# Attention with chunk selection and an MLP on one core: first loads in another buffer, chunk bounds by one strided reduction, another order

## The chip, the cores and the metric

The kernel runs on one core of a Trainium2 chip. The metric is the device time of one execution in microseconds (us). The core has five engines with a queue each: PE (matmuls; its weight loads are shown apart as PEld), DVE (VectorE), ACT (ScalarE), POOL (GpSimd) and SP (SyncE, which here issues DMAs alone). POOL and ACT issue a few DMAs too. Each engine runs its own queue in the order in which the program gives it, and waits at the head of that queue for what an instruction needs.

## What is computed

q, k and v have the shape (4 batches, 8 heads, 768 positions, 64) in float32. The keys are cut into 24 chunks of 32. Of each chunk the smallest and the largest value in each of the 64 dimensions are taken; they give an upper bound of any score in the chunk:

```
k_min, k_max = min / max of k over the 32 keys of a chunk
ub   = sum over d of max(q * k_min, q * k_max)       # chunks after the query's own: -1e9
keep = the 6 chunks of the largest ub for each query
attn = softmax over kept keys, not after the query, of q.k / 8
x    = attn @ v, heads side by side: (3072, 512)
out  = elu(x @ w_in) @ w_out                         # w_in (512, 2048), w_out (2048, 512)
```

## The kernel before, in words

**Work units.** The 3072 tokens are 8 units of 384. Units 0 and 1 hold the first halves of batches 0 and 1, mixed: in the code u = 0 (tags with "p") is the first 192 positions of both batches, u = 1 (tags with "s") is the next 192. Units 2 to 7 are second half of batch 0, second half of batch 1, and the halves of batches 2 and 3. A unit goes through loading, transposes, chunk bounds and selection (`select`), scores, exponentials and the product with v (`attend_pair` for units 0 and 1, `attend` for the others), division by the sum (`divide`) and a transpose (`turn`; a DMA transpose for units 2 to 7). Then `mlp` runs it through both weight matrices: 16 products with w_in of 384 columns (L881, ops h), ELU in three steps on ACT, POOL or DVE, and DVE (L888 e, L890 m, L894 g), and 12 groups of products with w_out (L905, ops o; the last tile at L861).

**The recording layer.** `Graph.op` records operations with the engines that may run them, what they read and write; nothing is issued then. The string ORDER, written out, gives the queue (first letter of a triple: P, A, D, G for POOL, S for SP) and the operation's number; PLACES gives the slot that each buffer takes, in the order of first use. An operation runs on the engine that ORDER names; waits come from what it reads, writes and overwrites. So the two strings fix all queues and all reuse of buffers. PE also gets products of zeros (op fill, L944) at places of ORDER: 40 of them.

**Loads.** `prep_pair` loads k and q of u = 0 and u = 1 and calls `load_v` for v; all of it lands in class f, 8 slots of 128x512 float32 (q and k tiles use 96 rows). `load_v` casts what landed into vext (`vcast`, L335 on POOL, L322 on ACT, L324 on DVE). `prep` loads the later halves: k, q of batches 0 and 1, and v, into f too; q of batches 2 and 3 goes in 32-wide blocks into class fx (4 slots of 128x768 float32), to be transposed by DVE at L589. The weights come through POOL's queue: `load_w_in` (L293, three parts: hidden columns 0 to 3, 4 to 7 and 8 to 15 of 16) and `load_w_out` (L299, four parts), straight into w_in_sb and w_out_sb.

**Chunk bounds.** For batches 0 and 1 keys are transposed on PE (L404, L554), and DVE reduces them in place in PSUM (L369). For batches 2 and 3 `bounds_batch` (its two batches have 8 rounds in all: two head groups times two halves of a chunk each) loads 96 rows, one for each head and chunk, of 16 keys x 64 dimensions into the single buffer kc. DVE then halves the keys: a minimum of 512 against 512 into a buffer t of class f (L486), a maximum of the same in place in kc (L489), then for each of the two a run of 256, 128 and 64 (L495), the last into km. The two halves are joined at L501, maximum less minimum is taken at L504, and a transpose on PE (L508) and copies put them into kst. `select` multiplies kst with q (L609) and finds the six largest on DVE (L620 to L637).

Of the kernel before, what the change touches and what calls it, by code (L numbers as in the profile page):

```python
# [9 lines left out]
AOT = mybir.AluOpType  # L10
# [8 lines left out]
D = 64  # L19
# [20 lines left out]
D01D00S0yG03A0uS0rA0sD09G0jG04S0tP0DS0WP0MD0gA0VA02G06G0iPjVPjXP1aS0vA0HS0xD0OS0ZS0+S0wG0cS0YD0n  # L40
P11G05S0XG0dG07G0-P0KD0ED12G0aA0LPjWG0kA15P0TD0NS2RS0BS2iG0bD1cA0QP1jD0qA0SG0mP1kP1hD1eA0UG0RD0F
PjZD1bS2fPj+A10P1pP1oPjYP18D13S0zPj-S2hA0CPk0Pk1P1uD19G0AP1zP1tD0lGmzP1vG0GD0PD1iA1xS2gPk3P1qPk2
P2JGmAA1rA1sS2QA2KA1wP2wG0pP1lPk4P2oP2BA2xD2CP1yPk6A1mA1nA2LP1DS2IS2vS2kS2OP1APk8A1CP20D2DD2sP1N
D2qD2pPk5A1BP1OP1ED1FP1SD2ND2tG0oGmBP33P29P1RD34G0eP1IP1HD1PP3gG08P1+D2EG2MG2uD1JD1GD1TD1KD1UA0J
PkaPkcP25G17G2AP26G0fP1XA2FA3hD1QD21A2yD27P2aP1LD2bA2HD2cD2zA1gS2PS4-G2rP1YP1VP3lD1ZD1-D28D22A1W
P2dD2ePkeD1MGmCG2SG2GP23A24A1fPmWPmKPm-Pn2D3mD3nD3pAmXAmLD3oGmMA3iD3qDmNAm+An3D3rD3sGn0Dn1G14PmG
PmOPmSPkgPnePnyPk7AmHDmIDn4G3tG0hAmTDmJDmUPnCG2lGmYAmPAnfDn5DmVP38D3vA0IDmQP3+AnzDmRP3JGngGmDAnD
Pk9DnhGmEP4FDnAG3jPn6A3cDnEA40A3KP2XAn7A2+D39S32G3uS2mDnBDmZDnFPnaD3aP3HPnuAnbA3ID2YPnqGn8P4jA4G
D2ZD35D2-PkiG1dD3bPnmAnrA3kG36A4kGnsP3wP41GmFDn9D3yG3eAnvA16G30A42S3fGnwD3xPnGS50P4lAnnA31DntGno
S57A2nP4DPnTD3APkkDnpPnMS4+PniA4mA3dD3LDnxG37PnUPnND3zS2TD3BPnHD3CA4EAnjA3EDncDnkG2jG3DG3GPkbDnl  # L50
P3NDndPkdG43P4aD4nA4bP3QPnID3FP3MP48S7UP3SD3OP4MD3PP44S2VG2UA3TP45PnVA3RD46P5rA4NSbCP4OP5fS4YD47
G4HA4PD5sA2WS4ZP4sD5gD3UA49PnWD4QP4JP4uP4IP4RPnJP3WP3VA5tA4tD3XS4XA4vP5QD3YP4pD4KAnXG4cD4LAnKP4S
P3ZS7LG4wP4oA5RA3-D4TG5TSnYD4qP5EA5FP4eS7IP4dP4yG5vP4xA5SP5xD4UD4fP4VP5kSawA5oD4gP4hSbuA4WPnOD4z
D5yD4rD4AA4iD5zP5JP4BG5qS55P58PkfPkmA5BD5GD5LD5aA4CPoNSavPotD5mPnPS53AouPo9PoFG5AAoOD59D5hD5lD5K
A5HDoPG5bGovG5nD5iAnQS5wD5MAoGA5cDowAoaA5NDoQSaGSnSGobDoHS7KSbrG5eS7SP5VSbzDoIPo5G5jPopA56PnZAo6
# [115 lines left out]
def kernel(  # L171
# [9 lines left out]
    nc = tc.nc  # L181
# [194 lines left out]
    def prep_pair(b, u, G):  # L376
# [617 lines left out]
```

## Time and profile before

| | us |
|---|---|
| median of 3 runs (lowest to highest) | 291.08 (290.72 to 291.61) |
| the profiled execution's own time | 290.3 |
| its span (first to last instruction) | 288.5 |
| PE busy, share of the span | 267.1 (93%) |
| DVE busy | 231.6 (80%) |
| ACT busy | 202.1 (70%) |
| POOL busy | 116.9 (41%) |

Times of the trace count from the start of the span. "x85" in a row is a count of instructions, the two numbers after the bar are the group's busy time in us and the mean of one instruction in ns, and what stands after the second bar is the engine's idle time just before them and what ended it. In rows of the DMA issues, the last number is the median time from issue to landing. The granted TensorE clock is 0.998 of full.

### The profile page before, as it was taken

The numbers are of one execution on the slowest core, as the hardware profiler recorded it, in microseconds if no ns is written. First come the engines' busy times: TensorE is split into PE (matmuls) and PEld (weight loads), VectorE is DVE, ScalarE is ACT, GpSimd is POOL, SyncE is SP. The second block draws the span as 40 slices with busy tenths as digits, with TensorE's granted clock in tenths as the row PEclk, the third lists the DMA queues.
The fourth block names the chain that finished last, engine by engine and source line by source line (L and its number), as shares of the span: only waits on it lengthen the run. The fifth ranks groups of instructions, "written<-read, shape, count | busy, mean of one in ns | idle before, by whom it ended". The sixth has DMA issues, their size and how long they took to land.

```text
span 288.5 us, 6864 instructions
## 1 busy us (share of the span) xinstructions
PE 267.1 (93%) x2404; PEld 161.9 (56%) x2404; DVE 231.6 (80%) x711; ACT 202.1 (70%) x453; POOL 116.9 (41%) x218
## 2 busy tenths in 40 slices
PE   2897889999999999998799999999999999999995
PEld 1565555685546765556465555664555455665553
DVE  2729898769989999999998999899789869442761
ACT  2457579487789889999289559993599259892611
POOL 5448366433844237722056336530556023400210
PEclk9999999999999999999999999999999999999999
DMA  8999999968966569997598268664370240012103
GB/s 162 189 186 202 203 199 197 214 139 189 222 132 134 134 147 215 181 242 144 130 213 186 44 148 202 109 122 97 94 179 2 57 110 0 16 50 66 74 3 109
DMA packets 119715, 39.25 MB, mean 136 GB/s; under 512 B 111104, under 2 KB 115456, under 8 KB 119680
## 3 DMA queue, kind: packets, MB, share of 16 engines
q1 hardware_dynamic: 114256, 34.09, 56.8%
q0 software_dynamic: 3696, 4.19, 8.8%
q10 hardware_dynamic: 1728, 0.52, 0.8%
q8 instruction: 19, 0.31, 0.5%
q14 instruction: 16, 0.13, 0.1%
HBM read 30.41 MB, written 6.29 MB: 127 GB/s over the span
## 4 chain that ended last, share of the span: by engine, by line
PE 52%; DVE 23%; DMA 9%; issue 6%; ACT 4%; POOL 3%; SPq 1%; ACTq 0%; DVEq 0%; POOLq 0%
PE bank L881 19%; PE bank L905 14%; DMA xt<-on 6%; PE bank L791 5%; DVE gT L894 5%; PE bank L842 3%; DVE on L655 3%; PE bank L609 2%; DMA f<-in_k_dram 2%; ACT pt L806 2%; DVE rhs L324 2%; POOL m L890 2%; DVE m L890 2%; DMA f<-in_q_dram 1%; PE bank L404 1%
## 5 line engine op out<-in xcount | busy, mean ns | idle before, releaser
L881 PE MATMUL bank<-xt,w_in_sb 128*128 128x384 bf16 x512 | 91.2, 326 | 4.9 <-DMA xt<-on 3.3
L905 PE MATMUL bank<-w_out_sb,gT 128*128 128x512 bf16 x368 | 90.3, 379 | 0.2 <-DVE gT L894 0.2
L888 ACT ACTIVATE e<-bank 128x384 f32<-128x384 f32 x128 | 60.8, 496 | 41.5 <-PE bank L881 34.1
L890 POOL TENSOR_SCALAR m<-e 128x384 f32<-128x384 f32 x85 | 45.1, 538 | 87.3 <-ACT e L888 77.9
L894 DVE SCALAR_TENSOR_TENSOR gT<-bank,m 128x384 bf16<-128x384 f32 x128 | 66.4, 547 | 11.0 <-POOL m L890 9.6
L881 PEld LDWEIGHTS <-w_in_sb 128*128 128x128 bf16 x512 | 49.5, 98 | 40.7 <-issue 8.8
L806 ACT ACTIVATE pt<-bank 128x384 bf16<-128x384 f32 (+1 forms) x144 | 67.9, 547 | 4.1 <-PE bank L791 3.2
L905 PEld LDWEIGHTS <-gT 128*128 128x128 bf16 x368 | 34.8, 97 | 33.9 <-issue 1.5
L791 PE MATMUL bank<-rhs,lhs 96*128 96x384 bf16 (+2 forms) x240 | 44.4, 293 | 0.3 <-DVE on L655 0.2
L791 PEld LDWEIGHTS <-lhs 96*128 96x128 bf16 x240 | 21.8, 97 | 14.4 <-issue 0.7
L823 POOL TENSOR_TENSOR pt<-pt,tri 128x256 bf16<-128x256 bf16 (+1 forms) x18 | 16.1, 899 | 26.6 <-ACT pt L810 20.2
L842 PEld LDWEIGHTS <-pt 128*128 128x128 bf16 x576 | 21.1, 97 | 4.6 <-DVE pt L823 0.7
L842 PE MATMUL bank<-vext,pt 128*128 128x65 bf16 x576 | 22.6, 193 | 0.6 <-DVE pt L823 0.6
L369 DVE TENSOR_REDUCE kst<-bank 128x12 f32<-128x384 f32 x32 | 16.6, 548 | 7.5 <-PE bank L404 7.3
L890 DVE TENSOR_SCALAR m<-e 128x384 f32<-128x384 f32 x43 | 17.6, 419 | 5.0 <-ACT e L888 4.8
L655 DVE TENSOR_TENSOR on<-bank,rcp 128x384 bf16<-128x384 f32 (+1 forms) x40 | 19.3, 497 | 0.8
L322 ACT ACTIVATE o<-bank 128x512 f32<-128x512 f32 (+1 forms) x16 | 8.7, 559 | 13.4 <-PE bank L905 10.5
L404 PE MATMUL bank<-ident_f,f 96*128 96x96 f32 x64 | 10.7, 313 | 7.6 <-POOL econst L278 4.3
L810 ACT ACTIVATE pt<-bank 128x512 bf16<-128x512 f32 x24 | 14.7, 614 | 1.6 <-PE bank L842 0.8
L404 PEld LDWEIGHTS bank<-ident_f,f 96*128 96x128 f32 x64 | 8.3, 180 | 10.8 <-POOL econst L278 4.3
L823 DVE TENSOR_TENSOR pt<-pt,tri 128x512 bf16<-128x512 bf16 (+1 forms) x30 | 12.6, 438 | 2.0 <-ACT pt L810 1.8
L653 DVE RECIPROCAL rcp<-bank 128x6 f32<-128x6 f32 (+1 forms) x40 | 7.2, 182 | 7.6 <-PE bank L842 3.7
(104 smaller groups left out, 330.3 us busy)
## 6 DMA issues: line engine op xcount, KB each, us to landing
f<-in_v_dram SPq DMA_DIRECT2D x22, 256.0 KB, 4.7
out_dram<-o SPq DMA_DIRECT2D x21, 256.0 KB, 2.5
f<-in_k_dram SPq DMA_DIRECT2D x18, 256.0 KB, 4.9
fx<-in_q_dram SPq DMA_DIRECT2D x32, 96.0 KB, 3.4
kc<-in_k_dram SPq DMA_DIRECT2D x8, 384.0 KB, 4.4
w_out_sb<-in_moe_w_out_dram POOLq DMA_DIRECT2D x4, 512.0 KB, 10.1
f<-in_q_dram SPq DMA_DIRECT2D x6, 256.0 KB, 4.1
f<-in_q_dram SPq DMA_DIRECT2D x6, 192.0 KB, 4.8
```

The costliest lines, as they stand in the source:

```text
L369: g.op(("kmin", "kmax")[w] + tag, (DVE,), lambda e, w=w, op=op: nc.vector.tensor_reduce(out=cs(w), in_=src(), axis=AX.X, op=op), reads=[(b ...
L404: nc.tensor.transpose(ap(bk)[:, c0:c0 + T96], ap(src[j])[0:T96, 256 * G + P * pr:256 * G + P * pr + P], ident_f[0:T96, 0:T96])
L655: g.op("on" + tag, (DVE,), lambda e: nc.vector.tensor_tensor(out=ap(on)[:, 0:nt].rearrange("p q h d -> p h q d"), in0=view()[:, :, :, 0:D] ...
L791: nc.tensor.matmul(ap(banks[hd])[:, o + pc:o + pc + wd], lhsT=apl(ls, G)[0:96, pr, hd, P * kb:P * (kb + 1)], rhs=ap(rs)[0:96, hd, c0 - HS ...
L806: lambda e, hd=hd, pt=pt, banks=banks, wtot=wtot: nc.scalar.activation(out=ap(pt)[:, hd, PAD:PAD + wtot], in_=ap(banks[hd])[:, 0:wtot], fu ...
L823: eng[e].tensor_tensor(out=view, in0=view, in1=tri[:, 64:64 + P].rearrange("p (a b w) -> p a b w", a=1, b=1) .to_broadcast([P, 2, len(dg), ...
L842: nc.tensor.matmul(view()[:, hd, qi, :], lhsT=ap(pt)[:, hd, P * qi + off:P * qi + off + P], rhs=ap(vx[b])[:, kb, 2 * r + hd, :], start=(kb ...
L881: nc.tensor.matmul(ap(bank)[:, 0:HS], lhsT=w_in_sb[:, kk, P * fc:P * (fc + 1)], rhs=ap(xT[i, kk]), start=(kk == 0), stop=(kk == NKK - 1))
L888: g.op(f"e{i}.{fc}", (ACT,), lambda e, eb=eb, bank=bank: nc.scalar.activation(out=ap(eb), in_=ap(bank)[:, 0:HS], func=AF.Exp), reads=[(ban ...
L890: g.op(f"m{i}.{fc}", (POOL, DVE), lambda e, eb=eb, mb=mb: eng[e].tensor_scalar(out=ap(mb), in0=ap(eb), scalar1=-1.0, scalar2=1.0, op0=AOT. ...
L894: nc.vector.scalar_tensor_tensor(out=ap(gt), in0=ap(bank)[:, 0:HS], scalar=0.0, in1=ap(mb), op0=AOT.max, op1=AOT.min),
L905: nc.tensor.matmul(ap(bank), lhsT=ap(gts[fc])[:, P * tt:P * (tt + 1)], rhs=w_out_sb[:, fc, :], start=(fc == 0), stop=(fc == NFC - 1))
```

## The change

Three edits, and new strings ORDER and PLACES.

1. w_out_sb gets a second use: eight pieces of 128x512 float32 of it become buffers w0 to w7. The first loads of v (u = 0) land in w0 to w3, the first loads of q (u = 0) in w4 to w7. The four loads of w_out now write those buffers too, so each waits until what landed there has been read: parts 0 and 1 for the casts of v of batch 0 and batch 1, parts 2 and 3 for the transposes of q of batch 0 and batch 1.
2. The loads of q for u = 1 land in fx instead of f, ahead of the q blocks of batches 2 and 3.
3. In `bounds_batch` two tensor_reduce instructions on DVE, one for the minimum and one for the maximum, read kc through a view with the 16 keys innermost (one element in 64), and write km. The buffer t of class f is no longer used there.

```diff
     w_out_sb = const.tile([P, NFC, DMODEL], BF16, name="w_out_sb")
+    stage = [Buf(f"w{i}") for i in range(8)]
+    for i in range(8):
+        store[f"w{i}"] = [w_out_sb[:, 2 * i:2 * i + 2].rearrange("p c n -> p (c n)").bitcast(F32)]
...
-                    writes=[(fixed, ("wo", i))], dma=True)
+                    writes=[(fixed, ("wo", i))] + [(stage[j], 0) for j in (2 * i, 2 * i + 1)]
+                    + [(stage[j], 1) for j in (2 * i, 2 * i + 1)], dma=True)
...
-                    ff[b, n, x] = buf = Buf(cls)
+                    ff[b, n, x] = buf = (stage[4 + 2 * b + x] if (n, u) == ("q", 0)
+                                         else Buf("fx" if (n, u) == ("q", 1) else cls))
...
-                load_v(f"{b}{'ps'[u]}{x}", b, kb, p0, p1)
+                load_v(f"{b}{'ps'[u]}{x}", b, kb, p0, p1, stage[2 * b + x] if u == 0 else None)
...
-    def load_v(tag, b, kb, p0, p1):
-        vf = Buf("f")
+    def load_v(tag, b, kb, p0, p1, vf=None):
+        vf = vf or Buf("f")
...
-                t = Buf("f")
-                g.op(f"kminc{tag}{y}a", (DVE,), lambda e, t=t, kc=kc: nc.vector.tensor_tensor(
...
-                g.op(f"kmaxc{tag}{y}a", (DVE,), lambda e, kc=kc: nc.vector.tensor_tensor(
...
-                        for n in (256, 128, 64):
-                            nc.vector.tensor_tensor(
...
+                for w, op in enumerate((AOT.min, AOT.max)):
+                    g.op(("kmin", "kmax")[w] + f"c{tag}{y}", (DVE,), lambda e, w=w, op=op, kc=kc, y=y, km=km:
+                         nc.vector.tensor_reduce(
+                             out=ap(km)[0:96, y, w], in_=ap(kc)[0:96].rearrange("p (w d) -> p d w", d=D),
+                             axis=AX.X, op=op), reads=[(kc, 0)], writes=[(km, (w, y))])
```

The new ORDER keeps the number of operations on PE (620, of them 40 fills) and the units in sequence, and shuffles within that. Counted from the two strings, operations that may run on several engines now stand elsewhere:

| operation | DVE before, after | ACT | POOL |
|---|---|---|---|
| m (L890) | 43, 29 | | 85, 99 |
| masks on pt (L749, L823) | 34, 26 | | 22, 30 |
| q into rhs (qa, L324) | 16, 10 | 19, 14 | 21, 32 |
| selection into rhs (mk, L324) | 15, 10 | 6, 4 | 11, 18 |
| v into vext (v) | 5, 6 | 12, 7 | 9, 13 |
| k into kt (kt, L324) | 2, 4 | 14, 12 | |

The one-hot constant (24 short memsets at L287) moves from DVE to POOL. In the first stage ACT issues 5 loads of k instead of 3. In SP's queue the last load of v for u = 0 (batch 0, positions 0 to 127) has 15 loads ahead of it in both orders, but more of u = 1 among them: q, k and v tiles, five instead of three. In POOL's queue the first load of w_in follows the cast of that v tile in both; the first load of w_out stands behind two copies of the selection (mk) where it stood ahead of all of them.

More of the change, by code (lines that the diff above doesn't have):

```diff
@@ L45 @@
[L45 to L50, printed above, removed]
@@ L120 @@
+150103160422601430627374172041021004106221010300721126502001323019470620421a5010702000124700c610
+211328152b1g000303125626102704041022d127001f1035325002400436227634011253230212156000354101210110
+27111622010e7520093352607ac21164202311851023b16012012413f20746372245271513g607040024103752136273
+657457003151211222674134165201126703100104563210070221d0510412081192602253a71011b061f22210040132
+22114e6017c6010
 """
```

154 lines of the change are left out of this document (72 added, 82 removed).

## The prediction

> **What bounds the kernel now.** I read the page first, then the busy times by stage, then the chain of work that ended last, and last the groups of instructions by shape.
>
> ```profile
> span 288.5 us, 6864 instructions
> ...
> PE 267.1 (93%) x2404; PEld 161.9 (56%) x2404; DVE 231.6 (80%) x711; ACT 202.1 (70%) x453; POOL 116.9 (41%) x218
> ```
>
> PE is busy for 267.1 of 288.5 us, and the change takes no matmul away (620 operations on PE in both orders, 40 of them fills). So it can only win back time in which PE stands idle, 21.4 us in all. The busy times by stage (columns: engine, busy us, instructions; last the share of the DMA engines) tell where that is:
>
> ```profile
> core 0: us, PE busy (x) PEld busy (x) DVE busy (x) ACT busy (x) POOL busy (x), PEclk, DMA share, GB/s
> 0.00:31.00 31.00, 21.08 (x210) 14.31 (x211) 18.16 (x72) 14.48 (x29) 15.70 (x38) 1.00 1.04 186
> 31.00:60.00 29.00, 27.51 (x245) 17.37 (x245) 24.18 (x81) 21.34 (x45) 15.52 (x29) 1.00 1.14 198
> 60.00:85.00 25.00, 24.73 (x228) 15.24 (x227) 22.57 (x75) 19.80 (x44) 13.14 (x26) 1.00 0.85 183
> 85.00:220.00 135.00, 129.70 (x1194) 77.48 (x1193) 125.34 (x372) 108.37 (x254) 58.66 (x102) 1.00 0.70 146
> 220.00:288.50 68.50, 64.08 (x532) 37.49 (x530) 41.35 (x115) 38.08 (x86) 13.85 (x25) 0.99 0.18 51
> ```
>
> PE's idle time is 31.0 - 21.1 = 9.9 us until 31, 1.5 from 31 to 60, 0.3 to 85, 5.3 from 85 to 220 and 4.4 after that. Two stages matter. Until 60 us the DMA share is 1.04 to 1.14: the transfers are one stream without holes, and what arrives when is a matter of their sequence. From 85 to 220 us DVE is the crowded engine: 125.3 of 135 us, while PE loses 5.3 us. All chunk bounds of batches 2 and 3 lie in that stage. A few places of the chain of work that ended last (start, length, what) show how it passes through the parts that the change touches:
>
> ```profile
> 87.22 0.52 ACT vext L322
> 87.77 2.88 DMA f<-in_k_dram
> ...
> 122.26 0.58 DVE f L486
> 122.86 0.70 DVE kc L489
> ...
> 134.74 1.20 DVE km L501 x2
> ...
> 140.14 3.74 DMA xt<-on
> ```
>
> At 87.2 ACT casts a v tile, and only then a k tile lands: the slot in f came free late, and the chain runs through the load. At 122 the chain runs through the first halvings of kc (L486, L489), at 134 through the join of the bounds (L501). At 140 it waits for a DMA transpose, which the change leaves.
>
> **The change part by part. First, the reduction.** Its rows, with the nearest other reductions and strided reads:
>
> ```profile
> L369 DVE TENSOR_REDUCE kst<-bank 128x12 f32<-128x384 f32 x32 | 16.6, 548 | 7.5 <-PE bank L404 7.3
> ...
> L486 DVE TENSOR_TENSOR f<-kc 96x512 f32<-96x512 f32 x8 | 5.7, 712 | 0.0
> L489 DVE TENSOR_TENSOR kc<-kc 96x512 f32<-96x512 f32 x8 | 5.7, 709 | 0.1
> ...
> L653 DVE RECIPROCAL rcp<-bank 128x6 f32<-128x6 f32 x24 | 4.3, 185 | 4.2 <-PE bank L842 3.7 <-ACT pt L810 0.3
> ...
> L620 DVE STREAM_TRANSPOSE ubT<-bank 128x384 f32<-128x384 f32 x8 | 4.3, 565 | 1.2 <-PE bank L609 1.1
> ...
> L495 DVE TENSOR_TENSOR kc<-kc 96x128 f32<-96x128 f32 x8 | 3.7, 466 | 0.3
> ...
> L495 DVE TENSOR_TENSOR f<-f 96x256 f32<-96x256 f32 x8 | 3.3, 416 | 0.0
> L495 DVE TENSOR_TENSOR kc<-kc 96x256 f32<-96x256 f32 x8 | 3.3, 415 | 0.1
> ...
> L495 DVE TENSOR_TENSOR f<-f 96x128 f32<-96x128 f32 x8 | 3.0, 374 | 0.3
> ...
> L653 DVE RECIPROCAL rcp<-bank 128x4 f32<-128x4 f32 x16 | 2.8, 178 | 3.4 <-PE bank L763 3.2
> ...
> L620 DVE STREAM_TRANSPOSE ubT<-bank 128x192 f32<-128x192 f32 x8 | 2.7, 364 | 1.0 <-PE bank L609 1.0
> ...
> L495 DVE TENSOR_TENSOR km<-f 96x64 f32<-96x64 f32 x8 | 1.8, 231 | 0.3
> ...
> L495 DVE TENSOR_TENSOR km<-kc 96x64 f32<-96x64 f32 x8 | 1.8, 221 | 0.3
> ```
>
> The eight rounds hold 8 instructions each: 712 + 416 + 374 + 231 ns for the minimum, 709 + 415 + 466 + 221 for the maximum, 3.54 us a round and 28.4 in all. After, a round has two reductions of 96 x 1024 elements. The trace has a reduction of 384 elements, without stride and from PSUM: 548 ns. What one more element costs is read from the transposes at L620: (565 - 364) / 192 = 1.05 ns. So one reduction takes 548 + 640 x 1.05 = 1220 ns if the stride costs nothing, 16 of them 19.5 us: DVE gains 8.9 us. No row shows a read from SBUF with one element in 64. The nearest rows with a stride are the reciprocals at L653, which read one float in 65 from PSUM: (185 - 178) / 2 = 3.5 ns for an element, although between 4 and 6 elements this may be noise. At 3.5 ns a reduction takes 548 + 640 x 3.5 = 2.8 us, 16 of them 44.6 us, 16.2 more than now. I see no reason for it to be below the contiguous price, so the bounds are -8.9 and +16.2 us of DVE time; I take -8.9, by the row that is the same instruction, and keep the other end.
>
> The Trainium skill speaks against this edit: "Advanced Engine Details and Errata", section SBUF Cachelines, says that lines are 16 bytes long and that a read with a new line for each access pays a penalty, which 64 floats between elements would bring. It gives no factor; the trace's row at 3.5 ns agrees in sign, but that one reads PSUM. On the other side "VectorE: DVE Perf Modes", section Mode 1× (REGULAR), describes that mode as one that takes float32 and odd strides alike, which gives the sum above. So the rule stands below as a rival.
>
> **Second, work that leaves DVE.** The new order hands instructions to POOL:
>
> ```profile
> L890 POOL TENSOR_SCALAR m<-e 128x384 f32<-128x384 f32 x85 | 45.1, 538 | 87.3 <-ACT e L888 77.9 <-DVE gT L894 5.2 <-ACT rhs L322 1.0
> ...
> L890 DVE TENSOR_SCALAR m<-e 128x384 f32<-128x384 f32 x43 | 17.6, 419 | 5.0 <-ACT e L888 4.8
> ...
> L324 POOL CAST rhs<-qt 64x384 bf16<-64x384 f32 x21 | 10.7, 516 | 1.1 <-ACT qt L322 0.4
> ...
> L823 POOL TENSOR_TENSOR pt<-pt,tri 128x256 bf16<-128x256 bf16 x12 | 9.3, 772 | 20.2 <-ACT pt L810 20.2
> L823 DVE TENSOR_TENSOR pt<-pt,tri 128x512 bf16<-128x512 bf16 x18 | 9.2, 512 | 0.2 <-ACT pt L806 0.2
> ...
> L823 POOL TENSOR_TENSOR pt<-pt,tri 128x512 bf16<-128x512 bf16 x6 | 6.9, 1154 | 6.5 <-ACT pt L806 6.4
> ...
> L324 DVE CAST rhs<-qt 64x384 bf16<-64x384 f32 x16 | 5.8, 363 | 0.2
> ...
> L823 DVE TENSOR_TENSOR pt<-pt,tri 128x256 bf16<-128x256 bf16 x12 | 3.9, 327 | 1.8 <-ACT pt L810 1.8
> ```
>
> 14 m x 0.419 = 5.9 us, 6 casts of q x 0.363 = 2.2, 8 masks x about 0.43 (the mean of the two DVE rows of L823) = 3.4, 5 copies of the selection, taken at the price of a cast, 1.8: 13.3 us less on DVE. One v and two kt more, taken at the 0.548 of a pass over 384 elements (L369), give 1.6 back. Net 11.7. With the reduction DVE falls from 231.6 to about 211 us. In the stage from 85 to 220, with its 8.9 and 125.3 / 231.6 of 11.7 = 6.3, DVE falls from 125.3 to about 110 of 135 us. POOL gains 14 x 0.538 + 8 x 0.96 (between 772 and 1154 ns, the two rows of L823) + 22 x 0.516 (11 casts of q, and 7 selections and 4 v at the same price) = 26.6 us and stands near 143 of 288: it has the room. But a mask on POOL takes 0.77 where DVE takes 0.33 us, and the product with v waits for it; what hides that is PE's other matmuls, as now. If that cover is gone, one such mask costs PE 0.44 us.
>
> **Third, the buffers.** Eight loads leave f for the space of w_out, four go to fx, and eight short uses of f (the t of each round) vanish: 20 uses of its 8 slots less. What it frees is a place like that at 87 us, where the chain waits for the landing (2.88 us in the chain). It costs nothing on any engine. The new waits of w_out are on casts of v and transposes of q that end before the first product with w_in at 31 us; behind the waiting DMA on POOL stand m and q casts. The products with w_out come after those with w_in and the three steps of ELU, so I cost these waits at nothing; without that cover a part of w_out that comes late costs PE its own delay.
>
> **Fourth, the first stage.** POOL's rows around the loads of w_in:
>
> ```profile
> 18.43 0.62 POOL L335 TENSOR_SCALAR vext<-f 128x512 bf16<-128x512 f32 x1 [5.13 <-DMA f<-in_v_dram]
> ...
> 21.95 0.74 POOL L293 DMA_DIRECT2D w_in_sb<-in_moe_w_in_dram  x1
> ```
> The landing row of the profile's DMA issues for that load, and PE in the same stretch:
> ```profile
> w_in_sb<-in_moe_w_in_dram POOLq DMA_DIRECT2D x1, 1024.0 KB, 13.6
> ```
> ```profile
> 31.09 4.71 PE L881 MATMUL bank<-xt,w_in_sb 128*128 128x384 bf16 x28 [0.38 <-DVE xt L324]
> ...
> 35.75 1.46 PE L881 MATMUL bank<-xt,w_in_sb 128*128 128x384 bf16 x8
> ```
>
> POOL casts the v tile at 18.43, as soon as it has landed; the w_in loads stand behind it. The last is issued at 21.95 and lands 13.6 us later, at 35.55. PE starts the first product with w_in at 31.09, runs seven groups of 4 (28 instructions), and goes on with the eighth at 35.75, so that landing is what it waits for; without it PE would have been there 0.3 us earlier. In the new order two more tiles of u = 1 lie ahead of that v tile. A full tile has 192 KB, and the stream moves 186 GB/s by the row of the first stage, so each is about 1 us and the cast and the w_in loads behind it come up to 2 us later. The new order answers with two transposes of k between h groups (L404, 8 instructions, about 1.1 us with their fills) and a row of seven fills ahead of the h groups that need the last part: PE has about 1 us more to do before it needs the landing. What is left is about 1 us of loss. In return the k and q tiles of u = 1 are there earlier for the work just after. I take +1.0 for the stage.
>
> **The sum.** In the crowded stage DVE has about 15 us more air. Not all of PE's 5.3 us there hang on it: the chain also waits for DMA transposes, as at 140 us. I take two thirds, -3.5 us, the place at 87 us among it. With +1.0 for the first stage that is -2.5: span 286.0, own time 290.3 - 2.5 = 287.8. The median shown, 291.08, lies 0.8 above the profiled execution, so I forecast 288.6 us.
>
> **The rivals.** (1) *The strided read is slow.* At twice the contiguous slope, 2.1 ns, a reduction takes 548 + 640 x 2.1 = 1.9 us, 16 of them 30.3 us: 1.9 more than before instead of 8.9 less. DVE's stage then stands at 110 + 10.8 = 121 of 135 us, nearly as full as now, but in an order laid out for a shorter one: the 5.3 us of PE stay, and each of the two batches comes late by what its 8 reductions exceed, 8 x 0.67 = 5.4 us, of which the air before the scores takes a part. I price it at 0 to +4: 290 to 295, middle 292.5. At 3.5 ns the stage has 110 + 25.1 = 135 of 135 us on DVE, which then sets its length; that gives 296 or more. For it speaks the row of L653; against it that L369 and the transposes keep one pace.
>
> (2) *The first stage gets longer: slower than before.* Place: the landing of the last w_in part, 35.55 now. PE's work ahead of it ends near 35.3 + 1.1 = 36.4 in the new order. From that point each microsecond of delay is a microsecond of the kernel, since the stream of transfers is full until 60 us and cannot catch up. With the v tile 2 us late and the w_in parts sharing the stream with three more tiles of u = 1 from SP's queue that get ahead of their last packets (3 us), the landing is at 40.5: 4 us lost, less 1.5 won back in the middle, 293.6. For it speaks the DMA share above 1 in the first two rows; against it that the sum of bytes is the same, so tiles that come earlier here are not in the way there.
>
> (3) *The change does not do what it frees.* If the slots of f held loads only where the stream was full anyway, and PE's 5.3 us in the crowded stage come from the DMA transposes and not from DVE, nothing is won or lost beyond the first stage: 290.5 to 292, middle 291.
>
> **How the numbers follow.** About 0.3% is what a measurement of this kernel can tell from no change, here 0.9 us: faster is below 290.2, slower above 292.0. The forecast (285 to 290) has a chance of 0.45. Rival 1 has 0.26: 0.22 at the double slope, of which 0.02 falls to faster and 0.05 to the same, and 0.04 at the far end. Rival 2 has 0.17, all slower. Rival 3 has 0.12: 0.03 faster, 0.07 the same, 0.02 slower. Together: faster 0.45 + 0.02 + 0.03 = 0.50, the same 0.12, slower 0.15 + 0.04 + 0.17 + 0.02 = 0.38. The low end is all 5.3 us of the middle and no loss at the head, 291.1 - 5.3, with a little for the end of the run: 285.0. The high end takes in rivals 1 and 2 but not the far end of the read's price: 295.5.
>
> **What would show it.** A row for the reduction of 96 x 1024 at about 1.2 us bears out the first step; 1.9 or more brings rival 1. DVE's busy time should be near 211 and POOL's near 143. In the stages from 85 to 220 PE's idle time should fall from 5.3 to below 2. The start of the eighth h group tells the first stage: near 37 as I have it, 40 for rival 2. The prediction is wrong if DVE is lighter as computed and PE's idle time in the middle has not moved: then the waits there were never DVE's.

## The result, and the profile after

| | before | after |
|---|---|---|
| median (lowest to highest), us | 291.08 (290.72 to 291.61) | 288.57 (288.00 to 289.74, 7 runs) |
| the profiled execution's own time, its span | 290.3, 288.5 | 288.57, 286.7 |
| ratio after to before, with its 95% interval | | 0.9926 [0.9899, 0.9953] |

The kernel became about 0.7% faster, and its median is the forecast's 288.6 within 0.1 us. The way there is another than forecast, though: one large term was mis-sized, and it is luck that other differences made up for it. Before ran seven times beside the changed kernel, with the same median; one of these runs, at 347.37 us, is slow and is left out of the ratio.

In the code after, the reductions are L491, m is L884, the masks L817, the division L649 (on), evictions and copies L325 (ACT) and L327, the products with w_in and w_out L875 and L899, the product with v L836, fills L938. The page's line of busy times, then the busy times by stage as in the prediction (engine, busy us, instructions):

```profile
span 286.7 us, 6781 instructions
...
PE 262.3 (91%) x2373; PEld 160.9 (56%) x2404; DVE 225.6 (79%) x608; ACT 195.9 (68%) x441; POOL 148.0 (52%) x285
```

```profile
0.00:31.00 31.00, 18.77 (x207) 14.10 (x209) 16.55 (x53) 13.48 (x28) 12.85 (x29) 0.94 1.19 187
31.00:60.00 29.00, 27.88 (x261) 17.88 (x264) 24.21 (x78) 19.98 (x43) 21.57 (x37) 1.00 1.15 204
...
85.00:220.00 135.00, 129.48 (x1191) 77.33 (x1205) 126.05 (x308) 101.73 (x236) 80.42 (x158) 1.00 0.70 144
```

Read the row 85 to 220 first: DVE is busy for 126.05 of 135 us (125.34 before, about 110 forecast), and PE idles 135 - 129.48 = 5.5 us (5.3 before, under 2 forecast). 31 matmul records are missing in this trace (2373, with 2404 weight loads), 14 of them in this stage (1191, with 1205), and they leave small gaps that look idle. Counting only PE's waits of over 0.2 us in its timeline, the stage has 0.55 + 0.66 + 1.36 + 0.31 + 0.56 + 0.64 = 4.1 us, and 4.8 before: they have moved, but by little. POOL stands at 148.0, near the 143 forecast; DVE's total is 225.6, not 211. The groups by shape say why:

```profile
L491 DVE TENSOR_REDUCE km<-kc 96x64 f32<-96x1024 f32 x16 | 30.5, 1918 | 0.1
...
L884 DVE TENSOR_SCALAR m<-e 128x384 f32<-128x384 f32 x29 | 13.2, 457 | 10.4 <-ACT e L882 10.2
```

A reduction takes 1.92 us and not 1.22: 30.5 us for the 16, where the halvings took 28.4. The rest of DVE's work fell by 6.0 + 2.1 = 8.1 us, where the prediction had 11.7. In part this is because instructions that stayed on DVE became longer: the 29 m take 457 ns each and not 419. Why they do is not shown. PE's waits from 85 to 235 us, picked from its timeline (start, length, what; in brackets the wait before it and its releaser), show where the crowding bites:

```profile
101.23 0.87 PE L548 MATMUL bank<-ident_f,f 128*128 128x128 f32 x6 [0.55 <-DVE on L649]
...
135.47 1.00 PE L836 MATMUL bank<-vext,pt 128*128 128x65 bf16 x27 [0.66 <-DVE pt L817]
...
141.42 2.92 PE L875 MATMUL bank<-xt,w_in_sb 128*128 128x384 bf16 x17 [1.36 <-DMA xt<-on]
...
196.24 0.85 PE L836 MATMUL bank<-vext,pt 128*128 128x65 bf16 x22 [0.56 <-POOL pt L817]
...
203.29 0.30 PE L502 MATMUL bank<-ident_f,km 96*128 96x96 f32 x1 [0.64 <-DVE km L498]
...
231.44 0.32 PE L875 MATMUL bank<-xt,w_in_sb 128*128 128x384 bf16 x1 [1.26 <-DMA xt<-on]
```

The two longest of them end with the landing of a DMA transpose, and so did the longest one before:

```profile
143.92 1.30 PE L881 MATMUL bank<-xt,w_in_sb 128*128 128x384 bf16 x7 [1.16 <-DMA xt<-on]
```

The chain that ended last, around the wait at 135.47, has a pair of reductions in it, and behind the pair the eviction, the division and the mask that PE waits for:

```profile
129.49 3.67 DVE km L491 x2
...
133.54 0.60 DVE o L327
...
134.28 0.56 DVE on L649
134.83 0.59 DVE pt L817
```

The first stage, in the row of the DMA issue and PE's timeline:

```profile
w_in_sb<-in_moe_w_in_dram POOLq DMA_DIRECT2D x1, 1024.0 KB, 16.1
```
```profile
31.35 0.85 PE L875 MATMUL bank<-xt,w_in_sb 128*128 128x384 bf16 x4
32.96 2.12 PE L875 MATMUL bank<-xt,w_in_sb 128*128 128x384 bf16 x12 [0.77 <-DMA w_in_sb<-in_moe_w_in_dram]
...
37.98 0.93 PE L938 MATMUL bank<-zeros 128*128 128x256 bf16 x7
38.74 0.39 PE L731 MATMUL bank<-rhs,lhs 96*128 96x128 bf16 x3
39.12 2.77 PE L875 MATMUL bank<-xt,w_in_sb 128*128 128x384 bf16 x16
```

The last part of w_in takes 16.1 us to land instead of 13.6, and the h groups that need it start at 39.12 instead of 35.75. But PE has other work in between (scores, transposes of k, fills), so that start alone tells no loss. The new wait is the one for the second part, 0.77 us at 32.96. Idle time doesn't measure a loss in this stage: in the first 31 us PE is busy for 18.77 us with 207 instructions, and for 21.08 with 210 before.

To compare orders that differ, I set each execution's weight loads, which are all recorded, beside the order of PE's operations, priced every kind of operation the same, and took the difference of the times at which two kernels have done the same work. This **lead** of the changed kernel over before (the time by which it is ahead), in the two executions above, is 0.9 us at 55 us, 1.4 at 81, 2.5 at 95, 1.8 at 108, 2.9 at 156, 1.2 at 201 and 1.7 at the end. The last is the difference of the own times, 290.3 - 288.57; the medians differ by 2.5. At 55 us the lead scatters: of six other kernels below whose first stage is the changed one's, four lead before's execution by 0.1 to 0.3 there and two trail it by 0.2 and 0.9; four kernels with before's first stage lie between 0.6 ahead of it and 1.0 behind. The mean of the executions with the changed first stage is 0.3 ahead of the mean of those with before's, which is not told from nothing. From 95 us on the lead goes up and down between 1.2 and 2.9, so it does not tell finely which later stretch won what.

### The profile page after: what moved, and what is told of

The parts are those of the page before. It is cut to its first block, busy times and chain, and to the rows that moved or that the text cites. A ratio compares the mean times of both kernels' runs of the same rounds, so it can differ in the third digit from the quotient of the medians.

```text
span 286.7 us, 6781 instructions
## 1 busy us (share of the span) xinstructions
PE 262.3 (91%) x2373; PEld 160.9 (56%) x2404; DVE 225.6 (79%) x608; ACT 195.9 (68%) x441; POOL 148.0 (52%) x285
## 4 chain that ended last, share of the span: by engine, by line
PE 48%; DVE 28%; DMA 9%; ACT 5%; issue 5%; POOL 2%; SPq 2%; DVEq 0%; ACTq 0%
PE bank L875 15%; PE bank L899 13%; DVE km L491 6%; PE bank L785 5%; DVE gT L888 4%; DMA xt<-on 4%; PE bank L836 3%; DMA f<-in_k_dram 3%; ACT e L882 3%; PE bank L603 2%; DVE on L649 2%; DVE kst L372 2%; PE bank L408 2%; DVE thr L622 2%; PE bank L548 2%
## 5 line engine op out<-in xcount | busy, mean ns | idle before, releaser
L875 PE MATMUL bank<-xt,w_in_sb 128*128 128x384 bf16 x512 | 92.7, 326 | 3.9 <-DMA xt<-on 2.6
L884 POOL TENSOR_SCALAR m<-e 128x384 f32<-128x384 f32 x99 | 52.7, 541 | 73.4 <-ACT e L882 57.0
L899 PE MATMUL bank<-w_out_sb,gT 128*128 128x512 bf16 x338 | 86.4, 379 | 1.8 <-issue 0.2
L875 PEld LDWEIGHTS <-w_in_sb 128*128 128x128 bf16 x512 | 49.1, 98 | 38.5 <-issue 6.2
L899 PEld LDWEIGHTS <-gT 128*128 128x128 bf16 x368 | 34.5, 97 | 34.7 <-issue 1.6
L785 PE MATMUL bank<-rhs,lhs 96*128 96x384 bf16 (+2 forms) x240 | 45.1, 293 | 0.4
L491 DVE TENSOR_REDUCE km<-kc 96x64 f32<-96x1024 f32 x16 | 30.5, 1918 | 0.1
L817 POOL TENSOR_TENSOR pt<-pt,tri 128x256 bf16<-128x256 bf16 (+1 forms) x24 | 21.8, 915 | 12.9 <-ACT pt L800 12.1
L325 ACT ACTIVATE o<-bank 128x512 f32<-128x512 f32 (+2 forms) x16 | 8.5, 542 | 25.5 <-PE bank L899 21.2
L836 PEld LDWEIGHTS <-pt 128*128 128x128 bf16 x576 | 20.9, 97 | 5.7 <-DVE pt L817 1.3
L836 PE MATMUL bank<-vext,pt 128*128 128x65 bf16 x576 | 22.7, 193 | 1.5 <-DVE pt L817 0.7
L327 POOL CAST rhs<-qt 64x384 bf16<-64x384 f32 x32 | 16.5, 519 | 10.7 <-ACT qt L325 5.8
L884 DVE TENSOR_SCALAR m<-e 128x384 f32<-128x384 f32 x29 | 13.2, 457 | 10.4 <-ACT e L882 10.2
L649 DVE TENSOR_TENSOR on<-bank,rcp 128x384 bf16<-128x384 f32 (+1 forms) x40 | 19.4, 498 | 0.8
L327 POOL COPY rhs<-selT 32x384 bf16<-32x384 bf16 (+1 forms) x18 | 11.7, 651 | 5.8 <-DVE selT L631 4.9
```

What stands on the lines that cost most here:

```text
L327: eng[e].tensor_copy(out=dst, in_=src)
L491: nc.vector.tensor_reduce(out=ap(km)[0:96, y, w], in_=ap(kc)[0:96].rearrange("p (w d) -> p d w", d=D), axis=AX.X, op=op), reads=[(kc, 0)], ...
L649: g.op("on" + tag, (DVE,), lambda e: nc.vector.tensor_tensor(out=ap(on)[:, 0:nt].rearrange("p q h d -> p h q d"), in0=view()[:, :, :, 0:D] ...
L785: nc.tensor.matmul(ap(banks[hd])[:, o + pc:o + pc + wd], lhsT=apl(ls, G)[0:96, pr, hd, P * kb:P * (kb + 1)], rhs=ap(rs)[0:96, hd, c0 - HS ...
L836: nc.tensor.matmul(view()[:, hd, qi, :], lhsT=ap(pt)[:, hd, P * qi + off:P * qi + off + P], rhs=ap(vx[b])[:, kb, 2 * r + hd, :], start=(kb ...
L875: nc.tensor.matmul(ap(bank)[:, 0:HS], lhsT=w_in_sb[:, kk, P * fc:P * (fc + 1)], rhs=ap(xT[i, kk]), start=(kk == 0), stop=(kk == NKK - 1))
```

## The experiments

Operations are shown by their names in place of ORDER's numbers. Each ratio is to the kernel before, run on the same chip at the same time; differences in us are those of medians.

**1. What does the stride cost?** The reductions read 16 neighbours:

```diff
-    in_=ap(kc)[0:96].rearrange("p (w d) -> p d w", d=D)
+    in_=ap(kc)[0:96].rearrange("p (d w) -> p d w", d=D)
```


> The changed kernel with the 16 reductions over 16 neighbours instead of one element in 64: same number of elements, wrong chunk bounds, so it selects other chunks. It tells what the stride costs, and whether DVE time in the crowded stage is worth anything. Price of the stride: if the contiguous price holds, the row falls from 1918 to about 1220 ns and DVE by 11 us. Theory 1 (the forecast's own term: two thirds of PE's idle time between 85 and 220 hang on DVE): 2 to 3.5 us below the changed kernel, 285 to 286.5. Theory 2 (the waits there are DMA transposes and PE's order): within 0.7 us of the changed kernel.

Measured: 284.32 us (283.94 to 285.63), ratio 0.9771 [0.9747, 0.9796]. The group of the reduction, and the stage from 85 to 220:

```profile
L491 DVE TENSOR_REDUCE km<-kc 96x64 f32<-96x1024 f32 x16 | 19.0, 1201 | 0.1
```
```profile
85.00:220.00 135.00, 133.09 (x1251) 80.12 (x1250) 120.43 (x318) 106.10 (x246) 83.45 (x165) 1.00 0.68 145
```

1201 ns stands against the 1220 that the prediction had worked out for a read without stride. So its price for the instruction was right, and its choice of the bound wrong: the stride adds 0.72 us to each of 16, 11.5 us of DVE, and these cost the kernel 4.3 us in the medians. PE idles 1.9 us in the stage, and the one wait of over 0.2 us that is left there is for a DMA transpose (1.61 us at 141.88). DVE's total is 215.7 us, where 211 was forecast with this price: what left DVE for POOL gave less than worked out.

**2. From which stride on?** One stride for each pair of reductions, in the order of the eight rounds:

```diff
+    st = (1, 2, 4, 8, 16, 32, 64, 64)[4 * (b - 2) + 2 * G + y]
-    in_=ap(kc)[0:96].rearrange("p (w d) -> p d w", d=D)
+    in_=ap(kc)[0:96].rearrange("p (a w s) -> p a s w", w=16, s=st)
```


> The changed kernel with another stride in each of the eight rounds: 1, 2, 4, 8, 16, 32, 64, 64 floats between the elements that are reduced (wrong bounds, so other chunks are selected). If the price comes from each access opening a new 16-byte line, 1 and 2 take about 1.2 us, 4 and more 1.9. If it comes with any stride, all but 1 take 1.9. If it grows with distance, 8 to 32 lie between. If it isn't the stride but 1024 elements from this memory, all take 1.9.

Measured: 289.11 us in one execution. DVE's timeline, its lines for strides of 1, 2, 4 and 64 floats in turn:

```profile
86.47 1.22 DVE L492 TENSOR_REDUCE km<-kc 96x64 f32<-96x1024 f32 x1
...
95.62 1.21 DVE L492 TENSOR_REDUCE km<-kc 96x64 f32<-96x1024 f32 x1
...
120.19 1.99 DVE L492 TENSOR_REDUCE km<-kc 96x64 f32<-96x1024 f32 x1
...
199.17 1.91 DVE L492 TENSOR_REDUCE km<-kc 96x64 f32<-96x1024 f32 x1
```

A step: 1.2 us up to 8 bytes from element to element, 1.84 to 2.03 from 16 bytes on, and no more at 256. That is what "Advanced Engine Details and Errata" of the Trainium skill states in SBUF Cachelines: lines of 16 bytes, two hits on a line hide the access, a new line for each access pays. The run adds the size, a factor of 1.6 for this instruction.

**3. The new order with the old halvings.** Each reduction is done by four halvings in a buffer that is no longer used at that time:

```diff
-    nc.vector.tensor_reduce(out=ap(km)[0:96, y, w], in_=..., axis=AX.X, op=op)
+    nc.vector.tensor_tensor(out=half, in0=ap(kc)[0:96, 0:512], in1=ap(kc)[0:96, 512:1024], op=op)
+    for n in (256, 128, 64):
+        nc.vector.tensor_tensor(out=half[:, 0:n] if n > 64 else ap(km)[0:96, y, w],
+                                in0=half[:, 0:n], in1=half[:, n:2 * n], op=op)
```


> The changed kernel, each strided reduction replaced by the four halvings of before (512, 256, 128, 64), in a buffer of its own. Theory 1 (the reduction at 1.92 us is about as dear as the halvings, so it neither brought nor cost much): a round is 2 x 1.73 us against 2 x 1.92, DVE 3 us lighter in all, time 0 to 1 us below the changed kernel, 287.5 to 288.6. Theory 2 (the reduction as such brought the gain): 290 or more. Theory 3 (the strided reduction cost the stage from 85 to 220 more than a microsecond): below 287.5.

Measured: 295.00 us (293.49 to 295.80), ratio 1.0138 [1.0108, 1.0169], 6.4 us slower than the changed kernel. Its groups, then the first halving's line (shortest, median and longest ns), then the worst place in DVE's, POOL's and PE's timelines:

```profile
L493 DVE TENSOR_TENSOR dead<-kc 96x512 f32<-96x512 f32 x16 | 13.5, 845 | 0.2
...
L496 DVE TENSOR_TENSOR dead<-dead 96x256 f32<-96x256 f32 x16 | 8.0, 503 | 0.6
...
L496 DVE TENSOR_TENSOR dead<-dead 96x128 f32<-96x128 f32 x16 | 6.5, 407 | 0.5
...
L496 DVE TENSOR_TENSOR km<-dead 96x64 f32<-96x64 f32 x16 | 5.4, 336 | 0.7
```
```profile
L493 DVE TENSOR_TENSOR dead<-kc x16: 644/686/2267, 87.0 to 208.0; 96x512 f32<-96x512 f32 x16
```
```profile
121.59 2.27 DVE L493 TENSOR_TENSOR dead<-kc 96x512 f32<-96x512 f32 x1
123.89 1.76 DVE L496 TENSOR_TENSOR dead<-dead 96x256 f32<-96x256 f32 x2
```
```profile
121.54 1.77 POOL L824 TENSOR_TENSOR pt<-pt,tri 128x512 bf16<-128x512 bf16 x2
123.37 2.14 POOL L328 COPY rhs<-selT 32x768 bf16<-32x768 bf16 x2
```
```profile
127.78 0.54 PE L792 MATMUL bank<-rhs,lhs 96*128 96x384 bf16 x3 [2.94 <-DVE gT L895]
```

The same halvings that took 28.4 us before take 33.4 here, since single ones are held up: 2.27 us for a first halving that takes 0.64 at its shortest, while POOL runs two masks beside it. The same place in the changed kernel, DVE and then POOL:

```profile
120.01 1.92 DVE L491 TENSOR_REDUCE km<-kc 96x64 f32<-96x1024 f32 x1
```
```profile
119.95 1.78 POOL L817 TENSOR_TENSOR pt<-pt,tri 128x512 bf16<-128x512 bf16 x2
121.80 1.68 POOL L327 COPY rhs<-selT 32x768 bf16<-32x768 bf16 x2
```

The reduction takes its mean there, with POOL busy all the while.

**4. Is it POOL that holds the halvings up?** Experiment 3 with four operations off POOL at this one place:

```diff
-G tri1103   G tri1104   G mk113   G mk112
+D tri1103   D tri1104   A mk113   A mk112
```


> The run with halvings in the new order, with two masks (128 x 512) of the group at 121.5 us handed from POOL to DVE and the two copies of the selection that follow them from POOL to ACT. Theory (a halving with both inputs in SBUF and POOL's reads of SBUF shut each other out): the first halving at this place falls from 2.27 us to 0.64 to 0.75, the pair of 96 x 256 from 1.76 to about 0.9, and of PE's wait of 2.94 us at 127.78 for DVE's gT more than half goes although DVE takes on 0.9 us of masks: the kernel is 1.5 to 3 us faster than the run with halvings alone (295.0), about 292.5. Rival (the halving was long there for another reason, such as the load of kc or the many instructions): its rows stay near 2.3 and 1.8 us, and with the masks on DVE the kernel is the same or slower, 295 to 296.

Measured: 290.65 us (289.13 to 291.20), ratio 0.9971 [0.9944, 0.9998], 4.35 us faster than experiment 3. DVE's and PE's timelines at the place:

```profile
121.32 0.68 DVE L493 TENSOR_TENSOR dead<-kc 96x512 f32<-96x512 f32 x1
122.03 0.74 DVE L496 TENSOR_TENSOR dead<-dead 96x256 f32<-96x256 f32 x2
```
```profile
123.93 0.76 PE L792 MATMUL bank<-rhs,lhs 96*128 96x384 bf16 x3 [0.69 <-ACT pt L807]
```

The first halving falls from 2.27 to 0.68 us, the next pair from 1.76 to 0.74, and PE's wait from 2.94 to 0.69, although DVE has taken on two masks. The gain is larger than expected (1.5 to 3 us). It is that of the whole edit: the first halving and the pair behind it become 1.6 + 1.0 = 2.6 us shorter, and the masks and copies run on other engines as well; how the rest divides isn't shown. "SBUF — State Buffer" of the Trainium skill, section Who interferes with whom, states the rule: a DVE instruction with two inputs in SBUF shares its second port with GpSimd's reads and one shuts the other out, while a reduction never does; the two runs and the reductions agree with both halves of it.

**5. The reductions in the old order.** Before, with the two reductions in the places of the halvings, the rest as it was:

```diff
-    nc.vector.tensor_tensor(out=ap(t)[0:96], in0=ap(kc)[0:96, 0:512], in1=ap(kc)[0:96, 512:1024], op=AOT.min)
+    nc.vector.tensor_reduce(out=ap(km)[0:96, y, w], in_=ap(kc)[0:96].rearrange("p (w d) -> p d w", d=D), ...)
```


> The kernel before with one part of the change alone: the strided reductions in place of the halvings (each at the place of its first halving), order, buffers and loads as before. Theory 1 (halvings read two operands and are held up when POOL is busy; the reductions are not, so they run through although they are 0.2 us dearer by their own time): at the place around 87 to 96 us PE loses less, 0.5 to 1.5 us below the kernel before, 289 to 290. Theory 2 (only DVE's busy time counts, and it grows by 16 x 1.92 - 28.4 = 2.3 us): 0 to 1.5 us above it.

Measured: 291.85 us (290.40 to 293.37), ratio 1.0011 [0.9983, 1.0038] (some bounds of batch 3 are overwritten before their use; the instructions are all there). Its group:

```profile
L487 DVE TENSOR_REDUCE km<-kc 96x64 f32<-96x1024 f32 x16 | 30.4, 1908 | 0.0
```

No difference, with 2.0 us more on DVE: there POOL is busy for 117 us, not 148, and the halvings were little held up (0.71 us for the first of a run, by the rows of L486 and L489). By itself this part of the change is worth nothing that can be measured. In the new order, with more on POOL, it is: 288.57 us with the reductions, 295.00 with the halvings.

**6. The place at 87 us: the k tile's slot?** Before, with the load of that k tile (ldk111) ahead of a v tile, and a slot freed for it:

```diff
 S ldq111
+S ldk111
 S ldv111
...
-S ldk111
```


> The kernel before with one slot of f freed in time: the k tile whose load waits for the cast at 87.2 us lands in the slot of the two halving buffers of that stretch (which move to constants that are dead by then), and its load goes ahead of the v load in front of it. Nothing else changes. Theory 1 (the shortage of f slots cost PE its 1.7 us between 87 and 95 us, and its end is a main part of the gain): 1 to 1.8 us below the kernel before, 289.3 to 290.1. Theory 2 (that wait is made up later, the gain is from elsewhere): within 0.5 us of the kernel before.

> As before_k111, with the slots of two later loads exchanged so that no tile is overwritten before it is read (in before_k111 one was, and PE stood 2.3 us at 99 to 102 us waiting for the load that overwrote it). In before_k111 the k tile landed at 85 instead of 92 us, and PE stood idle at 94 us as before. Theory 1 (the f slots made the gain): 1 us or more below the kernel before. Theory 2 (DVE, not the load, makes PE wait there): within 0.5 us of it.

Measured: the first form 293.39 us, ratio 1.0090 [1.0059, 1.0121]. In it another k tile (ldk200) and the minima of one round land in slots that are still read, so part of the bounds comes from other data, and PE waits for that tile by the edit's own doing (second line):

```profile
94.44 0.55 PE L556 MATMUL bank<-ident_f,f 128*128 128x128 f32 x3 [0.61 <-DVE o L326]
...
102.19 0.44 PE L556 MATMUL bank<-ident_f,f 128*128 128x128 f32 x2 [2.28 <-DMA f<-in_k_dram]
```

The second form has slots of its own: 290.33 us (289.65 to 293.27), ratio 0.9978 [0.9949, 1.0008], within the noise. In the first the k tile landed at 85.25 us instead of 92.26, and PE still waits 0.61 for DVE's eviction; in the second it waits 0.62 at 96.08. The wait that the chain showed at 87 us is not what PE loses there.

**7. The same place: DVE's queue?** Before, with two evictions of unit 1 on ACT:

```diff
-D oe1.0   D oe1.2
+A oe1.0   A oe1.2
```


> The kernel before with two evictions of unit 1's products with w_out (oe1.0 and oe1.2, 128 x 512, 0.68 us each on DVE at 91.85 and 94.33 us) handed from DVE to ACT; positions and slots stay. Theory (DVE's queue sets the loss of about 1.8 us that PE has at 87 to 96 us, and the k tile that came late there was hidden): DVE gets 1.36 us of air at that place, the wait of 0.62 us of the transposes of k at 95.06 for DVE's eviction is gone, and the kernel is 0.7 to 1.5 us faster than before, about 290.0 where before is 291.0. Rival (a buffer, a transfer or ACT sets that place): within 0.5 us of before, or slower by up to 1 us since ACT, busy for 13 of 15 us there, delays the exponentials.

Measured: 290.35 us (288.72 to 292.01), ratio 0.9958 [0.9928, 0.9988], 1.0 us faster in the medians. PE's timeline before, and here, where the transposes have no wait:

```profile
95.06 0.44 PE L554 MATMUL bank<-ident_f,f 128*128 128x128 f32 x2 [0.62 <-DVE o L324]
```
```profile
94.21 0.49 PE L554 MATMUL bank<-ident_f,f 128*128 128x128 f32 x3
```

In the lead, 1.0 us is won at this place against the same kernel a little earlier, and lost again by 150 us in that execution; among the later waits, that for a DMA transpose at 143.33 is 1.91 us. So DVE's queue sets the wait at this place, by what stands ahead of the eviction and not by a slot of f. That the 1.0 us of the medians comes from here is argued, not shown.

**8. Six m of unit 0 on POOL.** Before, with part of the new order's hand-over:

```diff
-D m0.0   D m0.2   D m0.14   D m0.15   D m0.8   D m0.10
+G m0.0   G m0.2   G m0.14   G m0.15   G m0.8   G m0.10
```


> The kernel before with six of the first unit's m instructions handed from DVE to POOL, as the new order has them (m of the hidden columns 0, 2, 8, 10, 14, 15); all queues else as before. Theory 1 (the first stage's gain of 1 to 2 us between 36 and 46 us is DVE's relief): PE loses 1 to 1.8 us less there, time 0.5 to 1.8 us below the kernel before. Theory 2 (it comes from the transfers and the sequence on PE): within 0.5 us.

Measured: 290.30 us (289.41 to 291.77), ratio 0.9960 [0.9936, 0.9983]: 0.7 us faster in the medians. The lead shows nothing up to 140 us in that execution, although all six stand before 60. The size agrees with relief of DVE; where it comes in isn't shown, and so the cause isn't either.

**9. w_in ahead of the v casts.** The changed kernel with the three loads of w_in earlier in POOL's queue:

```diff
 D pz
+G w_in0   G w_in1   G w_in2
 G rz
```


> The changed kernel with the three loads of w_in moved ahead on POOL's queue, before the casts of the two v tiles that they waited behind (issue near 17 instead of 21 us). In the changed kernel PE waits 0.8 us at 32 us for the second part and reaches the third one just as it lands, at 39.1 us. Theory 1 (rival 2 of the forecast: this landing is a bound): parts land 2 to 4 us earlier, 0.5 to 1.5 us below the changed kernel, 287.1 to 288.1. Theory 2 (the v and k tiles pushed back cost as much): the same or above 288.6.

Measured: 294.08 us (293.61 to 295.47), ratio 1.0083 [1.0050, 1.0116], 5.5 us slower than the changed kernel. PE's timeline:

```profile
32.57 0.74 PE L408 MATMUL bank<-ident_f,fx 96*128 96x96 f32 x3 [5.96 <-DMA fx<-in_q_dram]
```

The weights push the last q tile of u = 1 back: it lands at 32.53 us instead of 22.83, and PE waits 5.96 us for it. Here what w_in gains another load loses, and the late place of w_in is the better one.

**10. Less work on DVE, by ACT.** The changed kernel with eleven short instructions between 100 and 205 us on ACT:

```diff
-D oe1.1 kt110 oe2.2 qa0203 ky202 qr211 mk210 mk211 v300 oe4.0 qr300
+A oe1.1 kt110 oe2.2 qa0203 ky202 qr211 mk210 mk211 v300 oe4.0 qr300
```


> The changed kernel with eleven instructions of 0.3 to 0.7 us between 100 and 205 us handed from DVE to ACT (four evictions or casts of 128 x 512, and seven copies), about 5 us; positions and slots stay. Theory (DVE's time in the crowded stage is worth about 0.37 us of the kernel for each us, as the run with neighbours in place of strides gave, 11.5 us for 4.3, and ACT has room there): 1 to 2 us faster than the changed kernel, near 287. Rival (what ACT takes on stands in its queue ahead of exponentials and of the products' e, whose delay takes the place): within 0.7 us of the changed kernel or slower, 288 to 291.

Measured: 290.06 us (288.99 to 291.18), ratio 0.9948 [0.9920, 0.9976]: not faster than the changed kernel. The stage from 85 to 220, and two of PE's waits:

```profile
85.00:220.00 135.00, 129.74 (x1177) 76.62 (x1191) 120.37 (x295) 107.02 (x247) 79.92 (x160) 1.00 0.69 147
```
```profile
142.44 2.92 PE L875 MATMUL bank<-xt,w_in_sb 128*128 128x384 bf16 x17 [1.22 <-DMA xt<-on]
...
198.56 0.85 PE L836 MATMUL bank<-vext,pt 128*128 128x65 bf16 x22 [0.72 <-POOL pt L817]
```

DVE has 120.37 us in the stage, as in experiment 1 (120.43), and the kernel is some 6 us slower than that one. So DVE's total alone is not the measure, and my theory of 0.37 us of the kernel for each us of DVE falls. The waits at 142 and 198 stay. The rival, that ACT then delays others, isn't excluded: ACT has 107.02 us in the stage and not 101.73, and PE has new waits for ACT, 0.23 us at 119.05 and 0.33 at 171.28. One run can't tell relief that is worth nothing from relief that ACT takes back.

**11. The same work, in another order.** If what counts is what stands behind a pair of reductions, it must pay to let it pass. The changed kernel, with eleven operations moved within their queues:

```diff
 at  97 us:  kj200, kmin113, kj201 behind the division on013 (DVE)
 at 133 us:  mask tri1133 ahead of rcp112, on112; copies qa0203, ky202 behind on113 (DVE)
 at 194 us:  mask tri2134 ahead of the cast qa1302 (POOL)
 at 198 us:  eviction oe4.0 behind kj311 (DVE)
 at 222 us:  pv3030, pv3031 ahead of o5.0.2 (PE); mask tri3031 ahead of rcp301 (DVE)
```


> The changed kernel with eleven operations at other places in their queues, nothing else: at 97 us the joins of the bounds and one reduction of unit bounds (kmin113) behind the division on013; at 133 us the mask tri1133 ahead of the division of its neighbour, and two copies (qa0203, ky202) behind the division on113; at 194 us the mask tri2134 ahead of a cast on POOL that waits for DVE's transposes; at 198 us an eviction (oe4.0) behind the joins of the bounds; at 222 us the last products with v of a head group ahead of three groups of products with w_out, and their mask ahead of two reciprocals. DVE's work is the same to the instruction. Theory (what counts is not how long DVE is busy but what stands in its queue behind a pair of reductions of 3.7 us, which PE then waits for: 0.55 us at 101, 0.66 at 135, 1.36 at 141, 0.56 at 196, 0.64 at 203, 1.26 at 231): PE's idle time from 85 to 235 us falls by 2 to 4 us, and the kernel is 1.5 to 3 us faster than the changed one, 285.5 to 287. Rival (DVE's total is the bound there, so another order only moves the waits): within 0.7 us of the changed kernel, 288 to 289.3, with new waits of PE for DVE at other places.

Measured: 287.97 us (287.68 to 288.59), ratio 0.9895 [0.9871, 0.9920]. The stretch from 85 to 235 us, of the changed kernel and of this one:

```profile
85.00:235.00 150.00, 143.01 (x1314) 84.50 (x1330) 136.97 (x351) 108.90 (x251) 86.52 (x168) 1.00 0.66 138
```
```profile
85.00:235.00 150.00, 145.80 (x1341) 85.20 (x1340) 138.74 (x354) 110.64 (x254) 87.83 (x172) 1.00 0.64 138
```

By these rows PE's idle time falls from 7.0 to 4.2 us, with as much on DVE. But the changed kernel's trace lacks 16 matmul records in the stretch (1314, with 1330 weight loads), and this one lacks none. Counting waits of over 0.2 us alone, PE loses 3.2 us instead of 5.3. Those at 101, 135, 196 and 203 us are gone; at 141 us it still waits 1.30, and 0.37 is new at 149 and 0.51 at 202. The places came out as expected. The time did not: 0.6 us less than the changed kernel in the medians, and the two intervals overlap, so a gain over the changed kernel is not shown. In this execution PE is 1.3 us late at 90 us, before the first moved operation, and 0.4 ahead at the end: from there on it wins 1.7 us, near the 2.1 us of waits. It has the lowest median of the versions here that compute the reference in full; against before the gain is 1.05%.

## Why the time was right, and the steps not

**The reduction's price failed.** "16 of them 19.5 us: DVE gains 8.9 us ... I take -8.9, by the row that is the same instruction": it measured 30.5 and +2.1, within the bounds, and it is rival 1's price. The row that I took reads PSUM without a stride; experiment 1 confirms it for a read without stride, experiment 2 shows from which stride on it doesn't hold. The Trainium skill's rule stood in the prediction as a rival, with the right size: 1.9 us, 30.3 for all. That size was luck too: no row stood behind "twice the contiguous slope". The hand-over was mis-sized as well: "Net 11.7" measured 8.1.

**Rival 1 had the condition right and the price wrong.** It said "a reduction takes 548 + 640 x 2.1 = 1.9 us" and 292.5 us. As it said, PE's waits in the middle nearly stay; the "0 to +4" for batches that come late did not come, nor did the loss at the head. Why the lateness cost nothing isn't shown. What the prediction left out is how the two parts of the change hang together: it counted POOL's load as "it has the room" and did not price what it does to DVE. With halvings the new order takes 295.0 (experiment 3), and taking four operations off POOL at one place wins 4.35 us of that (experiment 4).

**"Two thirds, -3.5 us" in the middle failed as a sum.** PE's idle time from 85 to 220 went from 5.3 to 5.5, its waits of over 0.2 us from 4.8 to 4.1. What was won after the head lies, by the lead, between 55 and 108 us, 0.9 us in the two executions, the place at 87 us among it; the lead's ups and downs are as large as that. There the step "what it frees is a place like that at 87 us" named the wrong cause: experiment 6 frees the slot and wins nothing that can be measured, experiment 7 relieves DVE's queue, takes the wait away and wins 1.0 in the medians. From 108 us to the end nothing more was won on balance (a lead of 1.8, then 1.7). That -3.5 was sound for the price it was worked out from, experiment 1 shows: with a contiguous read the stage's idle time falls to 1.9, below the 2 that I named.

**"+1.0 for the stage" at the head** is not borne out: the eighth h group starts later, as described (39.12 against the 37 that I gave), but PE has enough else to do, and on the mean over executions it is 0.3 us ahead at 55 us, with a scatter of nearly 1 us either way. Rival 2 has its landing near 40 and not its loss. The step also read before wrongly: in its timeline PE has no wait between the first product at 31.09 and the eighth h group at 35.75, so that landing was not what PE waited for. The waits of w_out that I cost at nothing are not always nothing: in the changed kernel's execution the first product with w_out has no such wait, but in experiment 2's, with the same first stage, it has 1.60 us:

```profile
44.46 0.60 PE L901 MATMUL bank<-w_out_sb,gT 128*128 128x512 bf16 x2 [1.60 <-DMA w_out_sb<-in_moe_w_out_dram]
```

**The sum.** The forecast was +1.0 - 3.5 = -2.5. In the two profiled executions it is -0.9 at the head (of which the mean over executions bears out 0.3), -0.9 from there to 108 us, and nothing after: -1.7 by the unrounded leads, own time 288.57 where I forecast 287.8. The median after equals its profiled execution, while before's lies 0.8 above; that difference, which I had added, made the number come out, and that is luck. With the contiguous price the same kernel stands at 284.3, so the reductions' price, wrong by 4.3 us of the kernel, was met by errors the other way. The head's loss that didn't come is 1.3 of these; where the rest comes from isn't shown.

**"Wrong if DVE is lighter as computed and PE's idle time in the middle has not moved"** (the prediction's own test, shortened): idle time has hardly moved, but DVE wasn't lighter as computed either, so this test doesn't decide. Experiments 1 and 11 say more: shorter reductions leave one wait of over 0.2 us in the stage, and another order with the same work takes away four of the waits. So these waits are DVE's, directly or through POOL, and hang on what stands in the queues behind a pair of long reductions; experiment 10 shows that a lower total alone need not help. The wait at 141 us for a DMA transpose is another matter: it stays in all three (1.61, 1.30 and 1.22 us), so rival 3 has a part of PE's loss right. Why experiment 11 wins 0.6 us in the medians and 1.7 in its execution from 90 us on stays open; the scatter of the first stage can hide the difference.

## What to carry to other kernels

Price an instruction by a row with its own memory and its own stride, and when the trace has none, let the chances go by a rule that speaks against the nearest opcode's row rather than by that row. Before work goes to POOL, look at what DVE reads with two inputs from SBUF at the same time; a reduction that is slower by itself can be the faster one beside a busy POOL. And on a crowded engine ask not only how busy it is, but what stands behind its longest instructions and who waits for that.

## What the runs showed of the hardware

- tensor_reduce over 96 x 1024 float32 in SBUF: 1.17 to 1.22 us with 4 or 8 bytes from element to element, 1.84 to 2.03 with 16 to 256; a step and no slope (experiment 2).
- A tensor_tensor of 96 x 512 with both inputs in SBUF: 0.64 us at its shortest, 2.27 beside POOL's masks (experiment 3), 0.68 with these taken off POOL (experiment 4); and POOL's pair of copies beside the halvings took 2.14 us against 1.68 beside the reductions.
- Executions with the same first stage differ there by up to 1.8 us of PE's progress (0.9 ahead of before's to 0.9 behind it), more than the whole of some effects that were looked for.
